# Sparse attention and two expert layers on one core: three instead of five weight groups converted inside the attention, VectorE's extra operation moved between maxima and masks

## The chip, the cores and the metric

The kernel runs on one core of a Trainium2 chip. A core has TensorE (PE in the rows; PEld is its weight load), VectorE (DVE), ScalarE (ACT), GpSimd (POOL) and SyncE (SP, which here only issues transfers). Each takes its instructions in the order in which the program gives them to it. The metric is the device time of one execution in microseconds; less is better.

## The reference

Four sequences of 576 tokens, eight heads of 64. Attention with a threshold: only scores within tau of their row's maximum count. Then two dense layers in a row.

```python
scores = scale * np.matmul(q, k.transpose(0, 1, 3, 2))
thresh = np.max(scores, axis=-1, keepdims=True) - tau
scores = np.where(scores >= thresh, scores, -1000000000.0)
attn = np.exp(scores - np.max(scores, axis=-1, keepdims=True))
attn = attn / (np.sum(attn, axis=-1, keepdims=True) + 1e-09)
x = np.matmul(attn, v)                 # heads side by side: 2304 x 512
y = ((x @ w_a) * (x @ w_b)) @ w_out    # 512 -> 1536 -> 512
h = y @ w_in                           # 512 -> 1024
solu = h * softmax(h)
out = layernorm(solu) * g_ln @ w_out2  # 1024 -> 512
```

The weights come as 64-bit floats. Each is used as the sum of two 32-bit parts, a high and a low one, and so are x and the products between the layers: a product of two such pairs is three matmuls.

## The kernel before

**Weights.** They are cut into 52 pieces of 512 KB. A piece is loaded into a raw buffer (`wraw`, RB of them) and converted by six operations: exponent on ScalarE (`expo`, L128), three on VectorE (`low` L132, `sign` L135, `join` L138), the high part on ScalarE (`hi`, L142) and the low part on GpSimd (`lo`, L145). Three pieces make a weight group of the first layer (`w1`, twelve groups, one for each 128 hidden columns). Nine groups have room on chip: FW in a pool that lives all through (`wp`), the rest in a pool that takes the attention's memory when that is over (`wp2`). So 3 x FW pieces can be converted inside the attention. `conv_load` issues a load if fewer than RB are out; `conv_emit` emits the next operations of the piece in hand, as far as they belong to the engines it is given.

**Attention.** 16 head pairs of nine score tiles each. A step of the loop over `m` takes two tiles: a string of letters, PROG, gives the order in which the step's parts are emitted, and so the order on every engine. A and B: score products (L332), scaling with the row's minimum of the negated scores, that is the maximum of the scores (`soft_max`, L337 on VectorE), exponential (L349 on ScalarE). t and u: the thresholds (L354 on GpSimd). V: products with v of an earlier pair (L414). F: transpose of the reciprocals. T, U, Y: transposes of the step before (L383, L399, L402). a and b: the masks (L363 on VectorE, which also sum). f and z call `fill`, which emits what else VectorE has to do: operations of reciprocals first (`lo_old`, L369 and L370), else one VectorE operation of a conversion. From step 37 on the normalisation of the first block of x is fitted in too (`x_slots`, L228 and L234). The other conversion operations and the load stand at the step's end. Behind the last of 72 tile steps come six that only finish; in the first of them the first a/b product of the next layer is made.

**First expert layer.** The tokens are five blocks (512, 512, 512, 256 and 512 columns). It runs in units (block j, group f), first groups 0 to 5 for every block, then groups 6 to 11 for every block. A unit is `ab` (24 matmuls L256 into one of two PSUM buffers, then evacuated: a L595 on ScalarE, g L596 on VectorE, gt L597 on ScalarE and L598 on VectorE) and, two units later, `yacc` (12 matmuls L612). Behind each unit's `ab` and `yacc` its conversions are emitted, up to two pieces, and in two units of each block of the first pass the preparation of the next block's x: `prep_x` stage 0 (L211 on VectorE, L212 on ScalarE: normalise, high part) and stage 1 (L214 on VectorE: low part), for the last block `prep_x2` (L270, L271) for the second pass. `load_x` loads a block's x (L188) and reciprocals (L195). The units that prepare emit no conversion once groups 0 to 5 are converted.

**Second expert layer.** 18 token tiles; L698, a chain on the rows, transposes, L754. The first tile's split of y (`split_y`) is made near the end of the first layer.

Of the kernel before, what the change touches and what calls it, by code (L numbers as in the profile page):

```python
# [21 lines left out]
def kernel(  # L22
# [12 lines left out]
    NP, _, VS, D = v.shape  # L35
# [21 lines left out]
    NW = 9  # L57
    F1 = 6
    LAG = 2
    RB = 2  # L60
    FW = 5
    SCALE = 1.0 / float(D) ** 0.5
    BIG = 3.0e38
    EPS = 1e-9
# [20 lines left out]
    xr_p = ctx.enter_context(tc.tile_pool(name="xr", bufs=1))  # L85
    xh_p = ctx.enter_context(tc.tile_pool(name="xh", bufs=1))
# [192 lines left out]
    def attention():  # L279
# [181 lines left out]
        tot = NP * NS  # L461

        def fill(n):
            for _ in range(n):
                if lo_old:
                    lo_old.pop(0)()
                elif m in conv_at:
                    conv_emit(wstage, "D")
                    if m >= tot // 2:
                        conv_emit(wstage, "APD", 2)  # L470

        conv_at = [x for x in range(6, tot // 2 + 6) if x % 2 == 0 or x >= tot // 2]
        PROG = 'ABtVFTUYXaufbz'
        for m in range(tot // 2 + 6):
            if m == 30:
                load_x(0)
                x_slots = prep_slots(0)
            cur = [divmod(n, NS) for n in (2 * m, 2 * m + 1) if n < tot]
            old = [divmod(n, NS) for n in (2 * m - 2, 2 * m - 1) if 0 <= n < tot]
            lo_old, lo_q = lo_q, []  # L480
            pvs = [(j,) + PV[j % 2][m - j * NS // 2] for j in range(max(0, 2 * m // NS - 2), min(NP, 2 * m // NS + 1)) if m - j * NS // 2 in PV[j % 2]]
            mms = [f for p in pvs for f in pv(*p)]
            nm = {}
            th = {}

            def score(k):
                if k < len(cur):
                    nm[k] = sm.tile([P, 1], F32, name="nm")
                    scores(*cur[k])
                    soft_max(*cur[k], nm[k])  # L490
                    soft_exp(*cur[k])

            def thr(k):
                if k < len(cur):
                    th[k] = soft_thr(nm[k])

            def mask(k):
                if k < len(cur):
                    soft_mask(*cur[k], th[k])
                    if cur[k][1] == NS - 1:  # L500
                        recip(cur[k][0])

            def turn(k):
                if k < len(old):
                    tpose(*old[k])

            for ch in PROG:
                if ch in "AB":
                    score("AB".index(ch))
                elif ch == "V":  # L510
                    for mm in mms:
                        mm()
                elif ch == "F":
                    for j in range(NP):
                        if m - j * NS // 2 == 9:
                            finish(j)
                elif ch in "TU":
                    turn("TU".index(ch))
                elif ch == "Y":
                    for c in old:  # L520
                        tpose_tail(*c)
                elif ch in "tu":
                    thr("tu".index(ch))
                elif ch in "ab":
                    mask("ab".index(ch))
                elif ch == "f":
                    fill(1)
                elif ch == "X":
                    if m == tot // 2:
                        pre[0, 0] = ab_mm(0, 0)  # L530
                elif ch == "z":
                    fill(max(1, len(lo_old)))
                    if m >= 37 and m % 2 and x_slots:
                        norm_low, high = x_slots.pop(0)
                        norm_low()
                        if high:
                            evac_q.append(high)
            for fn in dma_q + later:
                fn()
            dma_q.clear()  # L540
            later.clear()
            i, s = divmod(2 * m, NS)
            r = m - (i * NS + 1) // 2
            if i < NP and r == 0:
                load_v(i)
                if i + 2 < NP:
                    alloc_qk(i + 2)
                    load_k(i + 2)
                    load_q(i + 2)
            for fn in pv_q + evac_q:  # L550
                fn()
            evac_q, pv_q = [], []
            if m in conv_at:
                conv_emit(wstage, "AP", 3)
                conv_load(wstage)
# [15 lines left out]
    def split_y(t, pool, tag="ys"):  # L571
        y = yt[t]
        ys = pool.tile([P, 2, KC, P], F32R, name="ys", tag=tag)
        nc.scalar.activation(out=ys[:, 0], in_=y, func=AF.Copy)
        nc.gpsimd.tensor_tensor(out=ys[:, 1], in0=y, in1=ys[:, 0].bitcast(F32), op=ALU.subtract)  # L575
        yt[t] = ys

    def moe1(wp2, ps_t):
# [49 lines left out]
        for n, (j, f) in enumerate(units):  # L628
            while f not in wst or conv["k"] < 3 * f + 3:
                conv_step(wstage)  # L630
            prevs.append((j, f, ab(j, f)))
            if len(prevs) > LAG:
                yacc(*prevs.pop(0))
            if n == len(units) - 4:
                load_y(0, xr_p, "zr")
                load_y(1, xr_p, "xr0")
            if n == len(units) - 2:
                split_y(0, xr_p, "xr1")
            limit = 3 * (NW + sum(u <= n - LAG for u in ends))
            prep = n < n1 and f in (2, 3)  # L640
            for _ in range(2):
                if conv["k"] < limit and (not prep or conv["k"] < 3 * F1):
                    conv_emit(wstage, "D")
                    conv_emit(wstage, "AP", 3)
                    conv_emit(wstage, "D", 2)
                conv_load(wstage)
            if n < n1:
                if n == 0:
                    load_x(1)
                if j + 1 < NBLK:  # L650
                    if prep:
                        prep_x(j + 1, f - 2)
                elif prep:
                    prep_x2(0, 2 * f - 4)
            elif f == F1:
                if j + 1 < NBLK:
                    load_x2(j + 1)
            elif f == F1 + 2:
                load_y1(j)
            elif f in (F1 + 3, F1 + 4) and j + 1 < NBLK:  # L660
                prep_x2(j + 1, 2 * (f - F1 - 3))
            for fn in later:
                fn()
            later.clear()
            if n < n1 and f == (F1 - 1 if j + 1 < NBLK else 0):
                if j + 2 < NBLK:
                    load_x(j + 2)
                elif j + 1 == NBLK:
                    load_x2(0)
# [186 lines left out]
```

## Time and profile before

| | us |
|---|---|
| median of 3 runs | 946.15 (946.12 to 947.04) |
| the profiled execution | 945.94 |
| its span in the profile | 944.1 |
| PE busy | 921.9 (98%) |
| PEld busy | 704.0 (75%) |
| DVE busy | 542.4 (57%) |
| ACT busy | 440.4 (47%) |
| POOL busy | 192.6 (20%) |

A busy TensorE here is one with matmuls between issue and modelled end, so a high share does not mean that it could not do the work faster. The shares are means over three stages (attention to about 281, first layer to about 724, second layer) in which different engines are loaded: VectorE is busy for around nine tenths in the attention and for around four tenths later. The granted clock of TensorE is 1.00 (2.4 GHz) until the last matmul.

### The profile page before, as it was taken

What the parts mean: (1) busy time and instruction counts of PE and PEld (TensorE: products, weight loads), DVE (VectorE), ACT (ScalarE), POOL (GpSimd) and SP (SyncE); (2) the same over time, 40 slices, a digit from 0 to 9 for tenths busy, and PEclk for the clock granted to TensorE, in tenths of its full rate; (3) what the DMA queues carried; (4) which work ended last, traced back from release to release, by engine and by line L of the source; (5) the groups of instructions that cost most, each with busy time, mean ns of one, the idle gap of its engine ahead of it and who ended that gap; (6) DMA issues with size and microseconds to landing.
All of it is one profiled execution on the core that took longest, in us unless ns stands there. A gap on an engine that the chain in (4) does not pass through costs nothing.

```text
span 944.1 us, 15070 instructions
## 1 busy us (share of the span) xinstructions
PE 921.9 (98%) x5680; PEld 704.0 (75%) x5680; DVE 542.4 (57%) x1169; ACT 440.4 (47%) x795; POOL 192.6 (20%) x292
## 2 busy tenths in 40 slices
PE   7999999999999999999999999999999999999998
PEld 3555555555567878889888888889988788888886
DVE  6898989999975754323147772222265544444443
ACT  5788887878763442213235432121232433333332
POOL 1111221212121220000013330000023433333330
PEclk9999999999999999999999999999999999999999
DMA  6443743463135474142115642022052111111100
GB/s 180 126 128 112 206 147 90 124 186 113 51 116 157 155 202 112 45 112 115 65 33 177 211 160 71 19 92 87 24 178 89 34 45 45 45 45 45 45 23 34
DMA packets 52616, 95.46 MB, mean 101 GB/s; under 512 B 12736, under 2 KB 28736, under 8 KB 49984
## 3 DMA queue, kind: packets, MB, share of 16 engines
q1 hardware_dynamic: 52112, 93.91, 32.1%
q8 instruction: 45, 0.74, 0.3%
q10 hardware_dynamic: 432, 0.59, 0.2%
q14 instruction: 27, 0.22, 0.1%
HBM read 70.80 MB, written 23.68 MB: 100 GB/s over the span
## 4 chain that ended last, share of the span: by engine, by line
PE 60%; DVE 3%; DMA 3%; ACT 2%; issue 1%; SPq 0%; POOL 0%; ACTq 0%; DVEq 0%
PE ps L256 26%; PE py L612 14%; PE po L754 10%; PE ps L698 9%; DMA wraw<-in_w_dram 2%; PE pl L735 2%; DVE g L596 1%; ACT gt L597 0%; DVE e L710 0%; DVE w L138 0%; ACT e L709 0%; DVE nm L706 0%; DVE xr L211 0%; ACT w L128 0%; ACT a L595 0%
## 5 line engine op out<-in xcount | busy, mean ns | idle before, releaser
L256 PE MATMUL ps<-xt,w 128*128 128x512 f32 (+1 forms) x1440 | 305.8, 368 | 1.9 <-DVE g L596 1.9
L256 PEld LDWEIGHTS ps<-xt,w 128*128 128x128 f32 x1440 | 251.4, 189 | 47.2 <-DVE g L596 2.3
L145 POOL TENSOR_TENSOR w<-w,w 128x512 fp32r<-128x512 f32 x52 | 76.8, 1478 | 413.5 <-ACT w L142 413.5
L612 PE MATMUL py<-gt,w 128*128 128x512 f32 (+1 forms) x720 | 157.5, 368 | 2.1 <-ACT y L616 2.1
L612 PEld LDWEIGHTS py<-gt,w 128*128 128x128 f32 x720 | 126.2, 189 | 25.0 <-ACT y L616 2.5
L596 DVE TENSOR_TENSOR g<-ps,a 128x512 f32<-128x512 f32 (+1 forms) x60 | 38.3, 638 | 180.7 <-ACT a L595 180.6
L349 ACT ACTIVATE pe<-ns,nm 128x576 f32<-128x576 f32 x128 | 94.0, 775 | 48.3 <-DVE ns L337 48.1
L595 ACT ACTIVATE a<-ps 128x512 f32<-128x512 f32 (+1 forms) x60 | 33.1, 552 | 178.2 <-PE ps L256 175.4
L363 DVE SCALAR_TENSOR_TENSOR pe<-ns,th,pe 128x576 f32<-128x576 f32 x128 | 102.7, 815 | 16.7 <-ACT pe L349 12.5
L337 DVE TENSOR_SCALAR_CACHE_REDUCE ns<-ps 128x576 f32<-128x576 f32 x144 | 102.7, 750 | 7.9 <-PE ps L332 7.8
L698 PE MATMUL ps<-w,ys 128*128 128x512 f32 x432 | 102.6, 393 | 1.6 <-POOL ys L575 1.4
L754 PE MATMUL po<-w,lt 128*128 128x512 f32 x432 | 101.4, 390 | 0.7 <-POOL lt L741 0.6
L332 PE MATMUL ps<-k,q 64*64 64x288 f32 x1152 | 91.2, 424 | 4.7 <-DMA k<-in_qkv_dram 4.4
L754 PEld LDWEIGHTS po<-w,lt 128*128 128x128 f32 x432 | 80.8, 188 | 18.1 <-POOL lt L741 1.1
L698 PEld LDWEIGHTS ps<-w,ys 128*128 128x128 f32 x432 | 79.8, 188 | 18.1 <-POOL ys L575 1.8
L414 PE MATMUL po<-pt,vr 128*64 128x322 f32 (+1 forms) x512 | 78.0, 419 | 1.7 <-ACT pt L376 0.9
L376 ACT ACTIVATE pt<-tp 128x512 f32<-128x512 f32 (+1 forms) x160 | 77.9, 545 | 0.2
L354 POOL TENSOR_SCALAR th<-nm,toff 128x1 f32<-128x1 f32 x144 | 38.4, 269 | 187.8 <-DVE ns L337 187.8
L383 PEld LDWEIGHTS tp<-ident,pe 128*128 128x128 f32 x512 | 55.9, 141 | 24.9 <-issue 9.4
L383 PE MATMUL tp<-ident,pe 128*128 128x128 f32 x512 | 70.9, 278 | 1.1 <-ACT pt L376 0.6
L414 PEld LDWEIGHTS po<-pt,vr 128*64 128x64 f32 x512 | 32.7, 136 | 42.5 <-issue 17.2
L332 PEld LDWEIGHTS ps<-k,q 64*64 64x64 f32 x1152 | 36.8, 134 | 32.8 <-DVE ns L337 7.8
(76 smaller groups left out, 807.6 us busy)
## 6 DMA issues: line engine op xcount, KB each, us to landing
wraw<-in_w_dram SPq DMA_DIRECT2D x36, 512.0 KB, 3.7
q<-in_qkv_dram SPq DMA_DIRECT2D x15, 576.0 KB, 4.1
k<-in_qkv_dram SPq DMA_DIRECT2D x30, 176.0 KB, 4.7
xd<-xp SPq DMA_DIRECT2D x16, 289.0 KB, 2.1
y<-yd SPq DMA_DIRECT2D x18, 256.0 KB, 3.0
vr<-in_v_dram SPq DMA_DIRECT2D x16, 256.0 KB, 3.7
xr<-xd SPq DMA_DIRECT2D x4, 1024.0 KB
zr<-rzd SPq DMA_DIRECT2D x8, 512.0 KB, 9.5
```

The costliest lines, as they stand in the source:

```text
L145: nc.gpsimd.tensor_tensor(out=w["o"][1], in0=w["f"] if wide else raw, in1=w["o"][0].bitcast(F32), op=ALU.subtract)
L256: nc.tensor.matmul(pa[:, 0:n], lhsT=wt[:, m, wi, kc * P:(kc + 1) * P], rhs=xt[:, kc, xi, :], start=(k == 0), stop=(k == 3 * KC - 1))
L332: nc.tensor.matmul(ps[t * D:(t + 1) * D, g, 0:HS], lhsT=q[r, u, c], rhs=k[r, u, o:o + HS], start=True, stop=True, skip_group_check=True)
L337: nc.vector.tensor_scalar(out=ns, in0=st[i, s][:, :, 0:HS], scalar1=-SCALE, scalar2=None, op0=ALU.mult, op1=ALU.min, accum_out=nm)
L349: nc.scalar.activation(out=pe.rearrange("p (g s) -> p g s", g=2), in_=ns, func=AF.Exp, bias=nm, scale=-1.0)
L363: nc.vector.scalar_tensor_tensor(out=pv, in0=ns, scalar=th, in1=pv, op0=ALU.is_le, op1=ALU.mult, accum_out=z[:, s:s + 1])
L376: evac_q.append(lambda: nc.scalar.activation(out=out, in_=in_, func=AF.Copy))
L383: nc.tensor.transpose(tp[:, kc, :], pe[:, o:o + P], ident)
L414: nc.tensor.matmul(po[h * D:(h + 1) * D], lhsT=lhsT, rhs=rhs, start=(kc == 0), stop=(kc == NQ), skip_group_check=True)
L612: nc.tensor.matmul(py, lhsT=wt[:, 2, wi, oc * P:(oc + 1) * P], rhs=gt[:, gi, :], start=(first and k == 0), stop=(last and k == 2))
L698: nc.tensor.matmul(ph[:, g, :], lhsT=y[:, a, kc, :], rhs=w2(2 * kc + g, b), start=(k == 0), stop=(k == 3 * KC - 1))
L754: nc.tensor.matmul(po, lhsT=lt[:, a, j, :], rhs=w2(2 * KC + j, b), start=(k == 0), stop=(k == 3 * NJ - 1))
```

## The change

Inside the attention three weight groups (nine pieces) are converted instead of five (fifteen), with three raw buffers instead of two. `fill` stands once in a step, between the maxima (and both thresholds) and the two masks, and emits at most one operation of a conversion, in every step from 6 on; before it stood behind the first mask and behind the second, in every other step. In the first expert layer the first four units convert up to three pieces each, and the preparation of the next x moves from units 2 and 3 of a block to units 4 and 5. The first y split of the second layer is written to another tile.

```diff
-    RB = 2
-    FW = 5
+    RB = 3
+    FW = 3
...
-        conv_at = [x for x in range(6, tot // 2 + 6) if x % 2 == 0 or x >= tot // 2]
-        PROG = 'ABtVFTUYXaufbz'
+        conv_at = range(6, tot // 2 + 6)
+        PROG = 'ABtuVFTUYXfab'
...
-                elif ch == "f":
-                    fill(1)
...
-                elif ch == "z":
-                    fill(max(1, len(lo_old)))
+                elif ch == "f":
+                    fill(len(lo_old))
                     if m >= 37 and m % 2 and x_slots:
                         norm_low, high = x_slots.pop(0)
                         norm_low()
                         if high:
                             evac_q.append(high)
+                    else:
+                        fill(1)
...
-                split_y(0, xr_p, "xr1")
+                split_y(0, xh_p, "xt")
...
-            prep = n < n1 and f in (2, 3)
-            for _ in range(2):
+            prep = n < n1 and f >= F1 - 2
+            for _ in range(3 if n < F1 - 2 else 2):
...
-                        prep_x(j + 1, f - 2)
+                        prep_x(j + 1, f - F1 + 2)
                 elif prep:
-                    prep_x2(0, 2 * f - 4)
+                    prep_x2(0, 2 * (f - F1 + 2))
```

VectorE in the attention, steps 10 to 12 (ns is the scaled score tile, pe the probabilities, wraw and wlow the piece in conversion). Before:

```order
L337 TENSOR_SCALAR ns,nm<-ps 128x576 x2
L363 SCALAR_TENSOR_TENSOR pe,z<-ns,th,pe 128x576
L132 TENSOR_SCALAR wlow<-wraw 128x512
L363 SCALAR_TENSOR_TENSOR pe,z<-ns,th,pe 128x576
L135 SCALAR_TENSOR_TENSOR wlow<-wraw,wlow 128x512
L337 TENSOR_SCALAR ns,nm<-ps 128x576 x2
L363 SCALAR_TENSOR_TENSOR pe,z<-ns,th,pe 128x576 x2
```

The same engine in steps 15 to 17 of the changed kernel:

```order
L337 TENSOR_SCALAR ns,nm<-ps 128x576 x2
L135 SCALAR_TENSOR_TENSOR wlow<-wraw,wlow 128x512
L363 SCALAR_TENSOR_TENSOR pe,z<-ns,th,pe 128x576 x2
L337 TENSOR_SCALAR ns,nm<-ps 128x576 x2
L138 SCALAR_TENSOR_TENSOR w_825<-w_825,wlow 128x512
L363 SCALAR_TENSOR_TENSOR pe,z<-ns,th,pe 128x576 x2
L337 TENSOR_SCALAR ns,nm<-ps 128x576 x2
L132 TENSOR_SCALAR wlow<-wraw 128x512
```

The extra operation moved from beside the second mask to the place between the maxima and the first mask, one in each step.

VectorE in the first expert layer, from the evacuation of unit 1 to that of unit 4 (g and gt are the unit's evacuation, xr and xt the next block's x). Before:

```order
L596 TENSOR_TENSOR g_4003<-ps,a_4002 128x512
L598 TENSOR_TENSOR gt<-g_4003,gt 128x512
L138 SCALAR_TENSOR_TENSOR w_3962<-w_3962,wlow 128x512
...
L596 TENSOR_TENSOR g_4055<-ps,a_4054 128x512
L598 TENSOR_TENSOR gt<-g_4055,gt 128x512
L203 TENSOR_SCALAR vs_3972<-vs_3972,neg 128x8
L211 SCALAR_TENSOR_TENSOR xr_3969<-xr_3969,vs_3972,zr 128x512 x4
L596 TENSOR_TENSOR g_4110<-ps,a_4109 128x512
L598 TENSOR_TENSOR gt<-g_4110,gt 128x512
L214 TENSOR_TENSOR xt<-xr_3969,xt 128x2x512 x2
```

In the changed kernel, from the conversions of unit 3 to the first product's evacuation of the next block:

```order
L138 SCALAR_TENSOR_TENSOR w_4127<-w_4127,wlow 128x512
L132 TENSOR_SCALAR wlow<-wraw 128x512
L135 SCALAR_TENSOR_TENSOR wlow<-wraw,wlow 128x512
L596 TENSOR_TENSOR g_4170<-ps,a_4169 128x512
L598 TENSOR_TENSOR gt<-g_4170,gt 128x512
L203 TENSOR_SCALAR vs_3922<-vs_3922,neg 128x8
L211 SCALAR_TENSOR_TENSOR xr_3919<-xr_3919,vs_3922,zr 128x512 x4
L596 TENSOR_TENSOR g_4221<-ps,a_4220 128x512
L598 TENSOR_TENSOR gt<-g_4221,gt 128x512
L214 TENSOR_TENSOR xt<-xr_3919,xt 128x2x512 x2
L596 TENSOR_TENSOR g_4276<-ps,a_4275 128x512
```

L211 moved behind unit 4's evacuation and L214 behind unit 5's; the next product evacuated (g_4276) is the one that reads xt.

SP, the loads at the start of that layer (wraw are pieces, xr and zr the second block's x and reciprocals). Before:

```order
L113 DMA wraw<-in_w_dram 128x1024
L188 DMA xr_3969<-xd_61 128x4x512
L191 DMA vs_3972<-xd_61 128x4x2
L195 DMA zr<-rzd_65 64x4x512 x2
L113 DMA wraw<-in_w_dram 128x1024 x2
```

In the changed kernel:

```order
L113 DMA wraw<-in_w_dram 128x1024 x2
L188 DMA xr_3919<-xd_61 128x4x512
L191 DMA vs_3922<-xd_61 128x4x2
L195 DMA zr<-rzd_65 64x4x512 x2
L113 DMA wraw<-in_w_dram 128x1024 x9
```

Two pieces stand ahead of the block's load instead of one, and nine behind it.

## Rows read from the trace of the kernel before

**Rows 1.** Timeline of VectorE in the attention: start us, us, what [idle before <-releaser].

```profile
109.19 0.69 DVE L138 SCALAR_TENSOR_TENSOR w<-w,wlow 128x512 uint32<-128x512 uint32 x1
...
113.69 0.75 DVE L337 TENSOR_SCALAR_CACHE_REDUCE ns<-ps 128x576 f32<-128x576 f32 x1
...
115.37 0.82 DVE L363 SCALAR_TENSOR_TENSOR pe<-ns,th,pe 128x576 f32<-128x576 f32 x1 [0.24 <-ACT pe L349]
...
117.93 0.74 DVE L337 TENSOR_SCALAR_CACHE_REDUCE ns<-ps 128x576 f32<-128x576 f32 x1
...
121.08 0.75 DVE L337 TENSOR_SCALAR_CACHE_REDUCE ns<-ps 128x576 f32<-128x576 f32 x1
```

**Rows 2.** Busy time by stretch: stretch, its length, each engine's busy us (instructions).

```profile
36.29:68.40 32.11, 32.11 (x315) 18.89 (x314) 29.02 (x82) 26.14 (x51) 6.01 (x19) 1.00 0.42 125
...
133.78:168.39 34.61, 33.49 (x316) 18.79 (x315) 31.91 (x86) 26.45 (x52) 5.80 (x19) 1.00 0.35 101
...
236.35:266.19 29.84, 28.97 (x284) 16.93 (x283) 27.26 (x77) 23.41 (x46) 5.50 (x17) 1.00 0.20 57
```

**Rows 3.** The chain that ended last: start us, us, what.

```profile
361.96 2.72 PE py L612 x12
364.68 5.44 PE ps L256 x24
```

**Rows 4.** Timeline at the seam, all engines.

```profile
280.93 11.14 PE L256 MATMUL ps<-xt,w 128*128 128x512 f32 x48
...
284.39 0.60 ACT L595 ACTIVATE a<-ps 128x512 f32<-128x512 f32 x1 [2.79 <-DMA rzd<-zt]
...
288.62 0.58 SPq L188 DMA_DIRECT2D xr<-xd  x1
...
290.10 0.58 ACT L595 ACTIVATE a<-ps 128x512 f32<-128x512 f32 x1
...
302.90 0.67 ACT L128 ACTIVATE w<-wraw 128x512 f32<-128x512 f32 x1 [5.95 <-DMA wraw<-in_w_dram]
...
303.46 0.59 ACT L595 ACTIVATE a<-ps 128x512 f32<-128x512 f32 x1
...
304.83 5.74 PE L256 MATMUL ps<-xt,w 128*128 128x512 f32 x24 [1.88 <-DVE g L596]
```

**Rows 5.** The same timeline at x's preparation and at the block change.

```profile
310.08 0.58 ACT L595 ACTIVATE a<-ps 128x512 f32<-128x512 f32 x1
...
312.69 2.35 DVE L214 TENSOR_TENSOR xt<-xr,xt 128x1024 fp32r<-128x1024 f32 x2
...
321.29 5.60 PE L256 MATMUL ps<-xt,w 128*128 128x512 f32 x24
...
345.30 3.06 PE L612 MATMUL py<-gt,w 128*128 128x512 f32 x12 [2.09 <-ACT y L616]
```

**Rows 6.** The same timeline in a unit that converts two pieces.

```profile
321.66 0.58 ACT L595 ACTIVATE a<-ps 128x512 f32<-128x512 f32 x1
...
324.27 0.68 DVE L138 SCALAR_TENSOR_TENSOR w<-w,wlow 128x512 uint32<-128x512 uint32 x1
324.99 0.63 ACT L142 ACTIVATE w<-w 128x512 fp32r<-128x512 f32 x1 [1.36 <-DVE w L138]
...
325.70 1.59 POOL L145 TENSOR_TENSOR w<-w,w 128x512 fp32r<-128x512 f32 x1 [2.84 <-ACT w L142]
326.25 1.60 DVE L138 SCALAR_TENSOR_TENSOR w<-w,wlow 128x512 uint32<-128x512 uint32 x1
...
328.98 0.58 ACT L595 ACTIVATE a<-ps 128x512 f32<-128x512 f32 x1
```

**Rows 7.** Timelines of ScalarE and VectorE in a later unit.

```profile
362.06 0.60 ACT L595 ACTIVATE a<-ps 128x512 f32<-128x512 f32 x1 [3.19 <-PE ps L256]
...
364.69 0.69 DVE L138 SCALAR_TENSOR_TENSOR w<-w,wlow 128x512 uint32<-128x512 uint32 x1
```

**Rows 8.** Busy time by stretch at the end; the number before the last two is TensorE's granted clock.

```profile
940.00:944.00 4.00, 0.12 (x1) 0.00 (x0) 0.00 (x0) 0.69 (x1) 0.00 (x0) 0.78 0.17 66
```

## The prediction

> **What bounds the kernel now.** The page has TensorE busy nearly all through, but its busy time runs to modelled ends, so I looked for the place where somebody waits, stage by stage: first VectorE's timeline inside the attention, then busy times by stretch, then the chain that ended last, then the timeline at the seam between attention and first expert layer.
>
> In the attention a step (two score tiles) has VectorE nearly without a break. A step with nothing extra lasts 3.15 us (117.93 to 121.08); the step before it, which carries two conversion operations, lasts 4.24 us (113.69 to 117.93). Each has one small hole: the first mask waits 0.24 us for the exponential [rows 1]. So VectorE sets the pace there. But TensorE stands close behind it. Nine steps (two head pairs) repeat in TensorE's work; the stretch 36.29:68.40 is one such period, from one step's score products to the same nine steps later, and in it TensorE is busy for 32.11 of 32.11 us. A later one takes 34.61 us [rows 2]; it holds the normalisation of x beside the conversions. I take 32.11 us as TensorE's own floor for nine steps, 3.57 per step.
>
> In the first expert layer TensorE is the bound: a unit is 5.44 us of a/b products and 2.72 us of y products, 8.16 together, one behind the other [rows 3]. It loses time at two places only: 1.88 us at 304.83 and 2.09 us at 345.30 [rows 4, 5]. Both come from a weight piece that landed late behind the block of x: the engine that waits for the piece also holds the unit's evacuation.
>
> **The change part by part.** Time zero below is the first product of the second unit (280.93 before) [rows 4]; the first unit's product is made inside the attention in both.
>
> *Attention.* Twelve pieces were converted between the steps before and three behind the last; now nine, one operation per step. From the first period's start to 266.19 there are 62 steps in 229.90 us [rows 2]; at the floor they take 62 x 3.57 = 221.2, so no more than 8.7 us is to be had. Where? The first three periods (36.29 to 133.78) take 97.49 against a floor of 96.33; there the new order puts an operation in every step. A piece costs VectorE about 1.09 us for its first two operations (4.24 less 3.15) and 0.69 for the join [rows 1]; three pieces (5.3), less nine waits of 0.24 now covered, on nine steps of 3.15, come to 31.5, just under the floor. So gain there is about nothing. The other 35 steps take 132.41 against 124.9. They keep only the eight x operations and have no conversion, so VectorE needs less than TensorE, and the 7.5 us should mostly come back. I take 6.5 in all, with 3 (two engines that stay within 2% of each other for 27 steps may hinder each other) and 8.7 as ends.
>
> *First expert layer, first block.* This is the large term. Units 0 to 3 now handle three pieces each, and the normalisation of the next x (an operation L203, four of L211) moves from unit 2 to unit 4, its low part (two of L214) from unit 3 to unit 5. All of this is queued on VectorE and ScalarE ahead of the next unit's evacuation a, g, gt. What a unit of two pieces costs these engines is seen from a to a: 321.66 to 328.98, 7.32 us [rows 6], under TensorE's 8.16. A third piece adds a join, a high part and the next exponent, which wait for each other: join 1.60, high 0.63, exponent 0.67 [rows 4, 6], about 2.9. Why 1.60 and not the 0.68 of a unit's first join: GpSimd's low part (325.70, 1.59 us) runs, and the join ends 0.56 behind it [rows 6]. No row shows a third join in one unit. The Trainium skill ("SBUF — State Buffer", Who interferes with whom) says that a VectorE operation with two SBUF inputs is blocked in full while a GpSimd operation reads SBUF; by it the third join is blocked as the second is. Without that it would cost 0.68, and the unit 9.3; I take 1.60, and 7.32 + 2.86 = 10.18 per unit.
>
> Now the starts of a, unit by unit. Unit 0: no wait for a store's landing any more (its tile lies elsewhere, behind the larger weight pool), so 0.7 instead of 3.46. Unit 1: 5.71 later for one join (284.39 to 290.10) plus 2.86 for the second, so 9.3. Unit 2: its queue holds the exponent of a piece whose load is now issued just behind the load of x; before, such a piece landed at 302.90, 14.3 us after the load of x was issued at 288.62 [rows 4]. The load of x goes out behind the second of two piece loads, and that waits for the second piece's sign operation: about when the next a started before, 5.71 after the first, so at 6.5, and x at 6.9. The piece lands at 21.2 and a starts 0.56 later (302.90, 303.46), at 21.75, not at 19.5. Unit 3: 31.9. Unit 4: 42.1. Then the four L211 and the high part come between: 303.46 to 310.08 before, 6.62, so unit 5 has its a at 48.7 [rows 4, 5]. Behind that unit's gt come the two L214, 2.61 us after a, 2.35 for both [rows 5]: the first is through at 52.5. The next product, of the second block, reads just that low part in its second matmul, so it starts at 52.3.
>
> Without any wait TensorE would be there at 5.44 + 4 x 8.16 = 38.08; before it was there at 40.36 (321.29) [rows 5] and lost 2.09 afterwards, which the third raw buffer should spare. So the term is 52.3 - 40.36 - 2.09 = 9.85 us more. Ends: 5 (third joins at 0.68 and the late piece in time) and 13 (the following pieces late as well).
>
> *The other block changes.* With the low part in unit 5 the next block's product waits at each of them. The a starts 0.10 after the product's end (361.96, 362.06), the operation behind gt 2.63 later (364.69) [rows 3, 7], the first L214 takes half of 2.35 [rows 5]: 3.9 us, against 2.72 of y products and 0.23 of the one matmul that needs the high part alone: 0.95 us. For the tail block of 256 columns about 0.4, into the block behind it about 1.05 (its y products take half as long), for the second pass 0.3, where the second of two halves is needed only six matmuls on. Together 2.7; ends 1.5 and 4.
>
> *The clock.* The granted clock is 1.00 through all these waits, and falls to a mean of 0.78 in 940 to 944, that is to its lower level (1.2 GHz) soon after the last product [rows 8]. A wait of some 11 us at the block change is far longer than any here. If the clock falls in it, the next products run at half speed for a while: between nothing and one unit's 5.44 us; I take 1.5. The skill ("TensorE: Matmul & The Clock Gate", the HAM clock gate) says that idleness throttles the array and activity releases it; by that this term is above nothing.
>
> *At no cost:* the third raw buffer (its loads go out earlier, and SP waits for VectorE in either case), the other place of the first y split (the tile it takes was last read by the tail block's units), conversions in the second pass (two per unit, as before).
>
> **The sum.** The profiled execution took 945.94 us (span 944.1 and 1.8 around it), 0.2 under the median of 946.15. 945.94 - 6.5 + 9.85 + 2.7 + 1.5 = 953.5.
>
> **The rivals.** *Both gains come, and the conversions keep up (faster).* It decides at the third piece: if it adds nothing to the 7.32 and the late piece is in time, a of unit 5 starts at 37.8 and the block change is at 41.4, about 1 us better than before's 42.45. Then 945.94 - 6.5 - 1.05 + 2.7 = 941.1. For it: VectorE's own operations of a piece take far less than 2.9 us. Against it: the two-piece unit, where the engines wait for each other and not for work [rows 6].
>
> *They cancel (no change).* The third piece adds nothing, but the piece behind the load of x is as late as before: unit 5's a at 43.5, the block change at 47.1, 4.65 worse; 945.94 - 6.5 + 4.65 + 2.7 + 1 = 947.8.
>
> *The attention gains nothing (slower still).* The denser operations make the first 27 steps longer by what the others gain, because masks stand later and the transposes of TensorE wait for them: 953.5 + 6.5 = 960. For it: TensorE waits for a mask in a few steps already. Against: these masks move by less than one operation, and the fewer conversions are certain.
>
> **Chances.** The forecast 0.62 (its own range 949 to 957), attention without gain 0.13, cancelled 0.12, faster 0.13. A measurement of this kernel tells 0.2% (1.9 us) from no change. Faster 0.13, same 0.12, slower 0.75. The range leaves out most of the fast case and the far end of the slow one: 946 to 960.5.
>
> **What would show it.** In the changed profile: periods of nine steps at about 32.1 to 32.6 all through, first masks that wait only in steps without an extra operation, and the attention ending some 6 us earlier; from the first unit's a onwards 8.6, 12.5, 10.2, 10.2 us between the a's; one wait of TensorE of about 11 us at the first block change, put down to L214 or L212, with waits of 1.4 and 2 us ahead of it, and waits of about 1 us at the later block changes; a granted clock below 1.00 around the first. I am wrong if a third piece costs a unit under 1 us, if that piece lands in time, or if the periods after step 36 stay near 34 us.

## The result and the profile after

| | before | changed |
|---|---|---|
| median (runs) | 946.6 us (4) | 958.17 us (4; 957.37 to 960.38) |
| ratio, 95% interval | | 1.0122 (1.0102 to 1.0143) |
| profiled execution, its span | 945.94, 944.1 | 958.05, 956.2 |
| start of the second unit's product ("time zero") | 280.93 | 273.86 |
| from there to the second layer's first product (L698) | 442.98 | 461.72 |

The change made the kernel 1.2% slower. The attention ends 7.07 us earlier; the first expert layer takes 18.74 us longer.

Timeline of the changed kernel, TensorE, ScalarE, VectorE and GpSimd, from time zero on; it answers to [rows 4 to 6]. Columns as there.

```profile
273.86 11.14 PE L256 MATMUL ps<-xt,w 128*128 128x512 f32 x48
274.44 0.57 ACT L595 ACTIVATE a<-ps 128x512 f32<-128x512 f32 x1
283.01 0.58 ACT L595 ACTIVATE a<-ps 128x512 f32<-128x512 f32 x1
...
285.62 0.69 DVE L138 SCALAR_TENSOR_TENSOR w<-w,wlow 128x512 uint32<-128x512 uint32 x1
287.05 1.59 POOL L145 TENSOR_TENSOR w<-w,w 128x512 fp32r<-128x512 f32 x1 [2.83 <-ACT w L142]
287.60 1.59 DVE L138 SCALAR_TENSOR_TENSOR w<-w,wlow 128x512 uint32<-128x512 uint32 x1
290.48 1.60 DVE L138 SCALAR_TENSOR_TENSOR w<-w,wlow 128x512 uint32<-128x512 uint32 x1
...
294.83 0.67 ACT L128 ACTIVATE w<-wraw 128x512 f32<-128x512 f32 x1 [2.09 <-DMA wraw<-in_w_dram]
295.41 0.57 ACT L595 ACTIVATE a<-ps 128x512 f32<-128x512 f32 x1
297.01 5.73 PE L256 MATMUL ps<-xt,w 128*128 128x512 f32 x24 [1.13 <-DVE g L596]
305.86 0.58 ACT L595 ACTIVATE a<-ps 128x512 f32<-128x512 f32 x1
307.21 5.74 PE L256 MATMUL ps<-xt,w 128*128 128x512 f32 x24 [1.75 <-DVE g L596]
316.05 0.58 ACT L595 ACTIVATE a<-ps 128x512 f32<-128x512 f32 x1
321.48 0.80 PE L256 MATMUL ps<-xt,w 128*128 128x512 f32 x1 [5.80 <-ACT xt L212]
322.65 0.58 ACT L595 ACTIVATE a<-ps 128x512 f32<-128x512 f32 x1
326.54 7.58 PE L256 MATMUL ps<-xt,w 128*128 128x512 f32 x23 [4.26 <-DVE xt L214]
...
378.92 5.51 PE L256 MATMUL ps<-xt,w 128*128 128x512 f32 x23 [1.05 <-DVE xt L214]
428.69 3.00 PE L256 MATMUL ps<-xt,w 128*128 128x256 f32 x23 [0.63 <-DVE xt L214]
460.00 7.15 PE L256 MATMUL ps<-xt,w 128*128 128x512 f32 x23 [2.43 <-DVE xt L214]
```

The six a's (L595) start 0.58, 9.15, 21.55, 32.0, 42.19 and 48.79 after time zero. TensorE waits 1.13 and 1.75 us for a unit's evacuation, then at the block change for the high part and again for the low part of the next x. The last three rows are the later block changes of the first pass.

Busy time by stretch, columns as in [rows 2]; first three periods of the attention (nine steps each, the last one eight), then the two places where the clock fell.

```profile
36.25:68.12 31.87, 31.87 (x316) 18.74 (x315) 31.30 (x85) 27.02 (x54) 10.52 (x20) 1.00 0.51 156
133.96:166.69 32.73, 32.08 (x316) 18.72 (x315) 30.15 (x82) 25.71 (x51) 6.85 (x20) 1.00 0.33 97
230.42:259.12 28.70, 28.70 (x284) 16.88 (x283) 25.07 (x72) 22.68 (x44) 4.24 (x16) 1.00 0.08 23
...
320.00:324.00 4.00, 0.80 (x1) 0.29 (x1) 2.35 (x4) 2.61 (x4) 0.00 (x0) 0.59 0.40 164
324.00:328.00 4.00, 1.46 (x4) 1.19 (x5) 2.96 (x3) 0.62 (x1) 0.00 (x0) 0.50 0.24 98
328.00:332.00 4.00, 4.00 (x13) 3.18 (x12) 0.00 (x0) 0.00 (x0) 0.00 (x0) 0.63 0.75 247
...
460.00:464.00 4.00, 4.00 (x11) 3.12 (x12) 1.08 (x1) 0.00 (x0) 0.00 (x0) 0.58 0.45 139
```

The period that took 34.61 us now takes 32.73, the last one 28.70 instead of 29.84. Behind both waits TensorE ran for a while at its lower clock: 23 matmuls took 7.58 and 7.15 us, where the same 23 took 5.51 at 378.92.

### The profile page after: what moved, and what is told of

The parts are those of the page before. It is cut to its first block, busy times and chain, and to the rows that moved or that the text cites. A ratio compares the mean times of both kernels' runs of the same rounds, so it can differ in the third digit from the quotient of the medians.

```text
span 956.2 us, 15055 instructions
## 1 busy us (share of the span) xinstructions
PE 925.0 (97%) x5680; PEld 707.1 (74%) x5680; DVE 547.0 (57%) x1169; ACT 439.9 (46%) x795; POOL 205.1 (21%) x292
## 4 chain that ended last, share of the span: by engine, by line
PE 89%; DVE 5%; ACT 3%; DMA 2%; issue 1%; POOL 0%; SPq 0%; DVEq 0%; ACTq 0%; POOLq 0%
PE ps L256 28%; PE py L612 13%; PE ps L698 10%; PE po L754 9%; PE po L414 9%; PE ps L332 8%; PE tp L383 7%; PE pl L735 2%; DMA wraw<-in_w_dram 1%; DVE w L138 1%; PE tq L399 1%; DVE g L596 1%; DVE xr L211 1%; ACT gt L597 1%; DMA k<-in_qkv_dram 1%
## 5 line engine op out<-in xcount | busy, mean ns | idle before, releaser
L256 PE MATMUL ps<-xt,w 128*128 128x512 f32 (+1 forms) x1440 | 311.4, 372 | 17.1 <-DVE xt L214 8.4
L145 POOL TENSOR_TENSOR w<-w,w 128x512 fp32r<-128x512 f32 x52 | 78.5, 1510 | 418.0 <-ACT w L142 418.0
L595 ACT ACTIVATE a<-ps 128x512 f32<-128x512 f32 (+1 forms) x60 | 33.1, 552 | 192.4 <-PE ps L256 192.4
L698 PE MATMUL ps<-w,ys 128*128 128x512 f32 x432 | 104.3, 398 | 1.7 <-POOL ys L575 1.4
L363 DVE SCALAR_TENSOR_TENSOR pe<-ns,th,pe 128x576 f32<-128x576 f32 x128 | 100.3, 814 | 7.9 <-ACT pe L349 5.6
L698 PEld LDWEIGHTS ps<-w,ys 128*128 128x128 f32 x432 | 81.0, 191 | 18.7 <-POOL ys L575 1.9
L354 POOL TENSOR_SCALAR th<-nm,toff 128x1 f32<-128x1 f32 x144 | 49.1, 343 | 182.5 <-DVE ns L337 177.0
L142 ACT ACTIVATE w<-w 128x512 fp32r<-128x512 f32 x52 | 33.0, 634 | 63.7 <-DVE w L138 63.7
```

What stands on the lines that cost most here:

```text
L145: nc.gpsimd.tensor_tensor(out=w["o"][1], in0=w["f"] if wide else raw, in1=w["o"][0].bitcast(F32), op=ALU.subtract)
L256: nc.tensor.matmul(pa[:, 0:n], lhsT=wt[:, m, wi, kc * P:(kc + 1) * P], rhs=xt[:, kc, xi, :], start=(k == 0), stop=(k == 3 * KC - 1))
L363: nc.vector.scalar_tensor_tensor(out=pv, in0=ns, scalar=th, in1=pv, op0=ALU.is_le, op1=ALU.mult, accum_out=z[:, s:s + 1])
L698: nc.tensor.matmul(ph[:, g, :], lhsT=y[:, a, kc, :], rhs=w2(2 * kc + g, b), start=(k == 0), stop=(k == 3 * KC - 1))
```

## The experiments

Theory: the loss is made in the first layer by the third pieces and by the late place of x's preparation, and the attention's gain is real. Rivals: one of the two alone; or the six pieces that the attention no longer converts cost their time wherever they are put. All runs in one table, with time zero and the length of the first layer from there, as above.

| run | median us | ratio to before (95%) | time zero | layer |
|---|---|---|---|---|
| changed, x's preparation early | 944.88 | 0.9988 (0.9977–0.9999) | 273.88 | 449.47 |
| changed, two pieces a unit | 950.78 | 1.0039 (1.0024–1.0053) | 274.63 | 454.19 |
| attention alone | 946.19 | 1.0007 (0.9993–1.0020) | 274.40 | 449.47 |
| layer alone | 970.38 | 1.0250 (1.0235–1.0264) | 281.04 | 466.84 |
| order alone | 943.82 | 0.9975 (0.9958–0.9991) | 276.46 | 444.62 |
| three groups alone | 955.78 | 1.0096 (1.0063–1.0129) | 279.63 | 455.14 |
| denser steps alone | 959.42 | 1.0123 (1.0097–1.0150) | 290.84 | 447.59 |
| order, three raw buffers | 937.03 | 0.9907 (0.9886–0.9928) | 275.98 | 438.43 |
| the same, four groups | 937.60 | 0.9904 (0.9885–0.9923) | 275.04 | 440.11 |
| changed, zeros for low parts | 955.89 | 1.0110 (1.0083–1.0137) | 273.92 | 459.80 |
| changed, x loaded early | 958.23 | 1.0122 (1.0105–1.0138) | 273.72 | 462.78 |
| changed, early at the tail | 954.46 | 1.0082 (1.0064–1.0101) | 273.91 | 457.52 |

**The two edits of the first layer, undone one by one.** x's preparation back in units 2 and 3:

```diff
-            prep = n < n1 and f >= F1 - 2
+            prep = n < n1 and f in (2, 3)
...
```

(The arguments of `prep_x` and `prep_x2` follow, as in the kernel before.)

> The changed kernel, with x's preparation back in units 2 and 3 of a block; three pieces in units 0 to 3 stay. Theory (both the third pieces and the place of the preparation cost): the waits at the later block changes go (6.9 us), so does the half clock behind the first (2.4), and at the first block change about 4 of 10 us come back, because the low part no longer stands between unit 5's a and the next product: 958.2 - 13 = about 945 (943 to 948). Rival (the third pieces alone make the loss): within 3 us of the changed kernel, 955 to 960.

Two pieces in each unit:

```diff
-            for _ in range(3 if n < F1 - 2 else 2):
+            for _ in range(2):
```

> The changed kernel, with two pieces in each unit; x's preparation stays in units 4 and 5. Theory: a's of the first block come every 7.3 to 8.2 us instead of 10.2, the first block change stands at about 45 after the second unit's product instead of 52.5, TensorE waits there about as long as at the later changes and keeps its clock; the later changes still cost 6.9: 958.2 - 7.2 - 2.4 = about 948.5 (946 to 951). Rival (the place of the preparation makes the loss at the first change too): 955 or more.

944.88 and 950.78: both totals as the theory had them, 13.3 and 7.4 us faster than the changed kernel. With the preparation early the waits at the later block changes are gone; the first block keeps one large wait, for a unit's g, and behind it the clock still fell, which the theory had not expected (24 matmuls in 7.65 us; TensorE, timeline):

```profile
312.95 7.65 PE L256 MATMUL ps<-xt,w 128*128 128x512 f32 x24 [6.68 <-DVE g L596]
```

With two pieces the block change comes 44.9 us after time zero (expected 45, changed 52.45). Two items were off: TensorE waits 4.56 us there and not about as long as at the later changes, and the clock still fell, so that 23 matmuls took 7.69 us (TensorE's timeline of that kernel):

```profile
319.75 7.69 PE L256 MATMUL ps<-xt,w 128*128 128x512 f32 x23 [4.56 <-DVE xt L214]
```

**Both undone, and both alone.** The attention's half: both diffs above on the changed kernel.

> The changed kernel with both edits of the first layer undone: the attention's half of the change, three raw buffers and the other place of the first y split stay. Theory: the attention's 7.1 us stay, nothing is lost in the first layer: 937 to 940, faster than before by 0.6 to 0.9%. Rival (the six pieces that the attention no longer converts are paid for in the first block in any case): 944 to 948.

The layer's half: the same two lines put into the kernel before.

> The kernel before with the first layer's half of the change alone: three pieces in units 0 to 3, x's preparation in units 4 and 5; five groups converted in the attention, two raw buffers. Theory: the third pieces and the late preparation cost the same with the attention unchanged: 945.9 + 12 to 20 = 958 to 966, and the attention's periods stay as before. Rival (the loss comes from the six pieces that were left over, not from where the first layer puts its work): within 4 us of before, 944 to 950.

The first went to the rival: 946.19, no faster than before. The attention's gain is there (time zero 274.40), and the first layer takes it back. No evacuation is late now; the products wait for the pieces themselves, their high part (L142) and low part (L145), as TensorE's timeline shows:

```profile
308.14 1.22 PE L256 MATMUL ps<-xt,w 128*128 128x512 f32 x2 [3.57 <-ACT w L142]
309.80 4.63 PE L256 MATMUL ps<-xt,w 128*128 128x512 f32 x10 [0.43 <-POOL w L145]
315.27 0.73 PE L256 MATMUL ps<-xt,w 128*128 128x512 f32 x2 [0.84 <-ACT w L142]
```

Its layer is 449.47 us long, and so is that of the kernel with three pieces and early preparation (one profiled execution of each; the medians are 1.3 us apart): with the preparation early it made next to no difference how the pieces were spread over the units. So my theory was short of a part: nine pieces left over for the first block cost time by their number. And the two edits of the first layer do not add up: undone singly they give back 13.3 and 7.4 us, together 12.0. The third pieces cost nothing while the preparation is early; they cost 7.4 us where the low part of x stands behind unit 5's evacuation, which they make late. The layer's half alone cost 24.5 us, more than expected (12 to 20), with only two raw buffers and with third pieces that five groups do not even need.

**What makes the attention's gain.** Order alone, on the kernel before (its FW, RB and first layer stay):

```diff
-        conv_at = [x for x in range(6, tot // 2 + 6) if x % 2 == 0 or x >= tot // 2]
-        PROG = 'ABtVFTUYXaufbz'
+        conv_at = range(6, tot // 2 + 6)
+        PROG = 'ABtuVFTUYXfab'
...
```

(The letter f then does what it does in the changed kernel, and z goes.)

> The kernel before with the attention's new order alone (one extra operation in each step, between the maxima and the masks); five groups, two raw buffers and the first layer as before. The run before this one showed that converting fewer groups is paid for in the first layer; so the question is whether the order alone keeps the attention's gain. Theory (order): a conversion costs VectorE 1.8 us in three steps, less the covered wait of 0.24 in each, so 3.15 + 0.6 - 0.24 = 3.5 per step, under TensorE's 3.54 (31.87 in nine steps): second unit's product at 274 to 275 instead of 281, total 938 to 941. Rival (it was the number of groups): product at 279 to 282, total 944 to 948.

Three groups alone, on the kernel before:

```diff
-    FW = 5
+    FW = 3
```

> The kernel before with three weight groups converted in the attention, in the old order; two raw buffers and the first layer as before. If the number of groups makes the attention's gain: second unit's product at 274 to 276, and the first layer then pays for the six pieces (7 to 10 us, two raw buffers): total 946 to 950. If the order makes it: product at 279 to 282 and the total 953 to 957.

Denser steps alone: the line of `conv_at` above, the letters as before.

> The kernel before with one part of the attention's new order alone: conversions in every step from the sixth on instead of every second in the first half; the string of letters, two places for an extra operation, five groups, raw buffers and first layer stay. Theory (the gain of the order comes from the operation that stands between maxima and masks and covers their wait, and from its being one per step): VectorE still waits some 15 to 17 us in all ahead of the masks, second unit's product at 279 to 282, total 944 to 948. Rival (it is the denser steps, which empty the second half of conversions): product at 275 to 277, total 940 to 943.

Order alone put time zero at 276.46, 4.47 us earlier than before: most of the gain, though short of the theory's 274 to 275, and 943.82 us lie between the two cases. Three groups alone came out as the case in which the order makes the gain: 279.63, 1.30 us earlier. Denser steps alone went against both: I had expected no change where the letters stay, and time zero came 9.91 us later. (The old line takes every second step up to step 71, not in the first half alone, as I had written; so this run puts up to two conversion operations into every step until the pieces are used up. TensorE's granted clock also fell there once, to 0.73 in 112:116.) The five answers that follow show groups by line, VectorE's masks from 30 to 275 us (count, busy us, mean ns; then the idle time ahead of them and what ended it). Before:

```profile
L363 DVE SCALAR_TENSOR_TENSOR pe<-ns,th,pe 128x576 f32<-128x576 f32 x116 | 93.2, 815 | 15.3 <-ACT pe L349 11.3 <-POOL th L354 4.0
```

The changed kernel:

```profile
L363 DVE SCALAR_TENSOR_TENSOR pe<-ns,th,pe 128x576 f32<-128x576 f32 x115 | 90.1, 814 | 6.8 <-ACT pe L349 4.7 <-POOL th L354 1.9 <-issue 0.2
```

Order alone:

```profile
L363 DVE SCALAR_TENSOR_TENSOR pe<-ns,th,pe 128x576 f32<-128x576 f32 x116 | 90.8, 812 | 3.9 <-POOL th L354 2.0 <-ACT pe L349 1.9
```

Three groups alone:

```profile
L363 DVE SCALAR_TENSOR_TENSOR pe<-ns,th,pe 128x576 f32<-128x576 f32 x116 | 92.9, 815 | 14.8 <-ACT pe L349 12.0 <-POOL th L354 2.7
```

Denser steps alone:

```profile
L363 DVE SCALAR_TENSOR_TENSOR pe<-ns,th,pe 128x576 f32<-128x576 f32 x114 | 92.0, 816 | 14.7 <-ACT pe L349 9.9 <-POOL th L354 4.7
```

Where the letters are old the wait stays at 15 us; where one operation stands between maxima and masks it falls to 4 to 7. Timeline of VectorE in the changed kernel: a step with one conversion operation (L135) lasts 3.45 us, and its first mask (116.03) waits for nothing.

```profile
114.07 0.75 DVE L337 TENSOR_SCALAR_CACHE_REDUCE ns<-ps 128x576 f32<-128x576 f32 x1
...
115.43 0.69 DVE L135 SCALAR_TENSOR_TENSOR wlow<-wraw,wlow 128x512 uint32<-128x512 uint32 x1
116.03 0.82 DVE L363 SCALAR_TENSOR_TENSOR pe<-ns,th,pe 128x576 f32<-128x576 f32 x1
...
117.52 0.74 DVE L337 TENSOR_SCALAR_CACHE_REDUCE ns<-ps 128x576 f32<-128x576 f32 x1
```

That is under TensorE's 3.54 us a step (31.87 in nine). With the old letters the wait stays and a conversion step can hold two operations, so VectorE needs more than TensorE; every second step without conversion had made up for it before, and the denser steps took these away. That last reading is argued from the step lengths, not tried by itself.

Where the gain lies, VectorE's timeline tells: the first maxima of steps 9, 36 and 63 start at 37.07, 135.13 and 238.24 before and at 37.57, 136.32 and 233.81 with order alone. So the first 27 of these steps gain nothing (98.75 us, 98.06 before), and the next 27 take 97.49 us instead of 103.11; in these steps the operations of x stand beside those of the conversions. The order moves the operations to another place and also spreads them evenly, at most one operation of a conversion or of x in a step. No run has one operation per step at the old place, so what the place alone is worth is not shown; the shorter wait ahead of the masks speaks for it.

The run with three groups is no full test of the number of groups: five of its nine joins still start at 130 us or later, in the changed kernel none. With the new order the number can be read by itself: time zero is 275.98 with five groups (order, three raw buffers) and 274.40 with three (attention alone), 1.6 us earlier.

**Keeping what gains.** The changed kernel with five groups and the first layer of before: new order, three raw buffers, the other place of the first y split.

```diff
-    FW = 3
+    FW = 5
```

> The changed kernel with five groups converted in the attention and the first layer of before (two pieces per unit, preparation in units 2 and 3): beside the order alone it has the third raw buffer and the other place of the first y split. Theory: the order's gain of 7 us, and TensorE's waits of 1.88 and 2.09 us for late pieces go: 935 to 938. Rival (the raw buffer gives nothing, since the loads behind x wait for the queue): within 1 us of the order alone.

The same with FW = 4:

> The fastest kernel so far (new order, five groups, three raw buffers, first layer as before) with four groups converted in the attention instead of five. Theory (nine pieces were too many for the first block, 50.7 us of VectorE's and ScalarE's chain against 38 of TensorE; six make 42, and the units run ahead by two): no wait of TensorE in the first layer or one below 1 us, second unit's product at 275 instead of 276: 935.5 to 937.5. Rival (every piece left over is paid for at about 1.1 us, as six cost 6.5): 939 to 941.

937.03 and 937.60: 1% faster than before, the fastest here, the second 0.1 us above the range of its theory (one wait of 1.09 us where none or one below 1 was expected). With five groups TensorE waits nowhere in the first layer's first block (its timeline, the products):

```profile
275.98 11.19 PE L256 MATMUL ps<-xt,w 128*128 128x512 f32 x48
289.73 5.60 PE L256 MATMUL ps<-xt,w 128*128 128x512 f32 x24
...
314.21 5.60 PE L256 MATMUL ps<-xt,w 128*128 128x512 f32 x24
```

Against order alone the layer is 6.2 us shorter; there TensorE had waited 3.54 us for a late piece and lost clock behind it (its timeline):

```profile
302.02 7.34 PE L256 MATMUL ps<-xt,w 128*128 128x512 f32 x24 [3.54 <-DVE g L596]
```

Both edits, the raw buffer and the place of the split, differ between the two, but the first y split waits as long in either (1.37 and 1.38 us), so I put the gain down to the third raw buffer; it was not tried by itself. With this first layer, three pieces left over are free of waits, six cost 1.7 us more (440.11 less 438.43), nine 11.0 more (449.47). Four groups give back in the layer what they gain in the attention.

**Three terms of the prediction, each by itself.** GpSimd writes zeros and reads nothing:

```diff
+            if 3 * FW <= k < 3 * FW + 12:
+                nc.gpsimd.memset(w["o"][1].bitcast(F32), 0.0)
+                return
```

> The changed kernel; for the twelve pieces of units 0 to 3 GpSimd writes zeros in the place of the low part and reads nothing (their low parts are left out of the result). Theory (a join is held up while GpSimd reads): the joins at 1.60 take 0.69, a third of a unit's chain goes: a's every 8.5 instead of 10.2 us, first block change at 47 instead of 52.5 after the second unit's product: 958.2 - 5.5 = 952 to 954. Rival (the time is in the engines waiting for each other, join, high part, exponent): joins stay at 1.60 or the a's intervals at about 10; 957 to 959.

The load of x ahead of the first unit (`load_x(1)` moved from the end of unit 0 to before the loop):

> The changed kernel, with the load of the second block's x issued ahead of the first unit instead of behind it. Theory (the third unit's a waits for a piece that lands late behind x): its a comes at 19.5 instead of 21.55 after the second unit's product, the block change about 2 us earlier: 955.5 to 957. Rival (the pieces behind x come late in any case, or the wait moves to the next link of the chain): within 1 us of the changed kernel.

The preparation early at the 256-column block alone:

```diff
-            prep = n < n1 and f >= F1 - 2
+            p0 = 2 if j == NBLK - 2 else F1 - 2
+            prep = n < n1 and f in (p0, p0 + 1)
...
```

> The changed kernel, with x's preparation back in units 2 and 3 for one block alone, the 256-column one, which prepares the block behind it; everything else as changed. Theory (the low part in units that last only 4.3 us, and the half clock behind the wait, make the 4.3 us of that block change): 958.2 - 4.3 = about 954 (953 to 955), no wait and full clock there, the other block changes as before. Rival (the block change is slow for another reason, such as the load of the next x): 957 or more.

The joins took 0.69 us without GpSimd's reads, as the theory said, and where no piece was late the a's came 8.0 to 8.7 us apart; but the total fell by 2.3 us only and lies between the two cases, because the exponent ahead of the third unit's a now waited 6.90 us for the late piece instead of 2.09. All twelve memsets, which wait for no operation of a conversion, ran in one go at the start, so GpSimd did nothing at all beside the later joins. Timeline of VectorE, GpSimd and ScalarE in that kernel:

```profile
274.08 6.23 POOL L146 MEMSET w<- 128x512 f32 x12 [12.24 <-PE po L417]
278.52 0.69 DVE L138 SCALAR_TENSOR_TENSOR w<-w,wlow 128x512 uint32<-128x512 uint32 x1
...
287.09 0.69 DVE L138 SCALAR_TENSOR_TENSOR w<-w,wlow 128x512 uint32<-128x512 uint32 x1
...
297.33 0.66 ACT L128 ACTIVATE w<-wraw 128x512 f32<-128x512 f32 x1 [6.90 <-DMA wraw<-in_w_dram]
```

Loading x earlier gained nothing (958.23): the wait moved to a piece before it, and the third unit's a came 22.3 us after time zero instead of the 19.5 of the theory. ScalarE there:

```profile
290.01 0.67 ACT L128 ACTIVATE w<-wraw 128x512 f32<-128x512 f32 x1 [3.19 <-DMA wraw<-in_w_dram]
```

I read this as one delay that x and the pieces share, so that their order only decides who has it; no run tries it further. At the 256-column block the theory held: 954.46, 3.7 us less, and the product behind that block no longer waits (TensorE's timeline):

```profile
457.39 5.63 PE L256 MATMUL ps<-xt,w 128*128 128x512 f32 x24
```

## Why the prediction was right, point by point

**Direction and mechanism.** Slower was forecast, at 953.5 and within 946 to 960.5, for the reason that the profile shows: a long wait of TensorE at the first block change (5.80 and 4.26 us with one matmul between them, about 11 forecast), put down to L212 and L214, behind waits of 1.13 and 1.75 us (forecast 1.4 and 2). The size was less good: 958.17 lies above the forecast's own 949 to 957 and nearer to the 960 of the rival in which the attention gains nothing; that rival is out because the attention did gain.

**Attention**, -6.5 forecast, -7.07 measured. The place was right: the first 27 steps take 97.71 us (97.49 before), the other 35 take 125.16 instead of 132.41. The reason was half wrong, so that the size agrees is in part luck. I gave the gain to the conversions that leave the second half; order alone, which leaves six of them there, gave 4.47 us, and three groups instead of five at the new order 1.6. The waits ahead of the masks that the new order covers were counted only for the first 27 steps, though they stand in all of them.

**First block**, +9.85 forecast. The block change is at 52.45 (the second matmul starts at 326.54, the one ahead of it counted with its 0.23) instead of 40.36, less the 2.09 lost afterwards before: +10.00. Each a was within 0.2 us of the forecast, and the third join took 1.60 us. "SBUF — State Buffer" (Who interferes with whom) of the Trainium skill says that a VectorE operation with two SBUF inputs contends with a GpSimd instruction that reads SBUF, not with one that only writes it. The traces agree with both: 1.60 us beside the low part, and 0.69 for the one join that ran beside a memset (at 278.52; the memsets ended at 280.31).

**The other block changes** is the step that was mis-sized: +2.7 forecast, 6.86 measured, from the starts of the same products in both traces (1.35, 0.88, 4.34 and 0.29 us for 0.95, 0.4, 1.05 and 0.3). The one behind the 256-column block was wrong, and it is most of what the forecast missed: I priced the wait for L214 against the half-length y products, and not that the four L211 and the second high part of a 512-column block (453.35 to 457.1) no longer fit into a unit of 4.3 us, so that the a ahead of L214 itself came late, at 457.08. The lower clock behind it added 1.6 us of the 4.34 (7.15 less 5.51). Timeline of VectorE and ScalarE there:

```profile
453.35 2.73 DVE L211 SCALAR_TENSOR_TENSOR xr<-xr,vs,zr 128x512 f32<-128x512 f32 x4
...
456.11 1.06 ACT L212 ACTIVATE xt<-xr 128x1024 fp32r<-128x1024 f32 x1 [0.26 <-DVE xr L211]
457.08 0.37 ACT L595 ACTIVATE a<-ps 128x256 f32<-128x256 f32 x1
...
458.72 2.35 DVE L214 TENSOR_TENSOR xt<-xr,xt 128x1024 fp32r<-128x1024 f32 x2
```

**The clock**, +1.5 forecast for the first block change, 2.07 measured (7.58 less 5.51).

**The sum.** -7.07 + 10.00 + 6.86 + 2.07 = 11.86; the profiled executions differ by 12.11. The first layer is 0.2 us shorter than its terms, which was not traced. The second layer is 0.44 longer: at its start the clock fell in the changed kernel and not before, which is shown further below. (In the rival that cancels, the 43.5 for unit 5's a is half a us more than the terms beside it give, 21.75 + 2 x 7.32 + 6.62 = 43.0; nothing hangs on it.)

**What the forecast did not see** is that the change loses for a simpler reason too: at the new order and with the first layer of before, three groups instead of five cost 9.2 us (946.19 against 937.03), more than the attention gains. The late preparation adds 4.6 to it (950.78), the third pieces 7.4 (958.17); in the other order of adding it is nothing for the third pieces (944.88) and 13.3 for the late preparation. The third raw buffer, put at no cost and credited with 2.09 us, is probably worth more: with the first layer of before about 6.2.

## What to carry to other kernels

Look in the busy engine's timeline for a short wait that comes back in every step, and put work that has to be done anyway into it: one operation per step between maxima and masks was worth 4.5 us here (its place and the even spread together), while up to two per step behind the masks cost 10. Work that is taken out of one stage has to fit the slack of the next, counted up to the first product that needs it: three pieces fitted, six nearly, nine did not, however they were spread. And an operation that the next block needs is not to stand behind the last unit's evacuation; where units are short, it has to stand further ahead.

## What the runs showed of the hardware that was not expected

The length of a wait did not by itself decide TensorE's clock. Behind the 256-column block the same wait of 2.43 us was followed by 23 matmuls in 7.15 us in the changed kernel, and in 5.55 in the kernel with zeros for low parts, at a granted clock of 0.58 and of 1.00 in the same stretch. Timeline and busy time by stretch of the latter:

```profile
459.75 5.55 PE L259 MATMUL ps<-xt,w 128*128 128x512 f32 x23 [2.43 <-DVE xt L217]
```

The clock stands ahead of the last two numbers:

```profile
460.00:464.00 4.00, 4.00 (x18) 3.24 (x18) 0.83 (x1) 0.00 (x0) 0.00 (x0) 1.00 0.55 170
```

At the start of the second layer it is the same with a shorter wait: 1.41 us are followed by 22 matmuls in 6.91 us in the changed kernel (granted clock 0.85 and 0.73 in 748:756), 1.42 by 5.29 in the one with x's preparation early and 1.37 by 5.28 before. TensorE's timeline, the changed kernel first:

```profile
749.89 6.91 PE L698 MATMUL ps<-w,ys 128*128 128x512 f32 x22 [1.41 <-POOL ys L575]
```

With x's preparation early:

```profile
737.67 5.29 PE L698 MATMUL ps<-w,ys 128*128 128x512 f32 x22 [1.42 <-POOL ys L575]
```

Before:

```profile
738.18 5.28 PE L698 MATMUL ps<-w,ys 128*128 128x512 f32 x22 [1.37 <-POOL ys L575]
```

The wait there is 1.36 to 1.42 us in all fourteen kernels; in five of them the granted clock fell behind it, in nine, the kernel before among them, it stayed at 1.00. One kernel also differs from execution to execution: the four of three groups alone have a mean granted clock of 0.990, 0.990, 0.994 and 0.996 and take 956.96, 956.77, 954.79 and 953.35 us.

The longest waits of the first layer were all followed by the lower clock, from the 3.54 us of order alone to the 6.68 with x's preparation early; shorter ones went either way. "TensorE: Matmul & The Clock Gate" (The HAM clock gate) of the Trainium skill says that the array's default state is throttled and activity releases the throttle. The rows agree with the release: behind the first block change, with products running, the granted clock goes from 0.50 (324:328) over 0.63 (328:332) to 1.00 (332:336). No run here shows what decides between the two cases of equal waits.
